# Loads of q and k in rows of eight tokens, longer zero matmuls, and new engine choices and orders

## The chip, the cores and the metric

The kernel runs on one core of a Trainium2 chip. Its engines work side by side, each through its own list of instructions in order: PE (TensorE, matrix products; PEld is its weight load), DVE (VectorE), ACT (ScalarE), POOL (GpSimd) and SP (SyncE, which here issues nearly all DMAs). They meet through semaphores. The metric is the device time of one execution in microseconds (us); lower is better. A profiled execution gives the durations; "span" is the time from its first to its last instruction.

## The reference

Two layers, one behind the other, with B = 4 batches, H = 8 heads, S = 768 tokens, D = 64:

```python
scores = q @ k.T / sqrt(D)                   # per batch and head
keep = (pos_k < 4) | ((0 <= pos_q - pos_k) & (pos_q - pos_k < 128))
a = softmax(where(keep, scores, -1e9))       # 4 sink keys and a window of 128
x = (a @ v), heads side by side              # [B, S, 512]
x_prev = x shifted by one token, zero first
xk = mu_k * x + (1 - mu_k) * x_prev          # xr likewise with mu_r
kk = relu(xk @ w_k) ** 2                     # 512 -> 1024
out = sigmoid(xr @ w_r) * (kk @ w_v)         # [B, S, 512]
```

Inputs and outputs are float32; products run in bfloat16 and sum in float32.

## The kernel before

**Units.** The work is cut into 12 units of 256 tokens: unit u is batch u // 3 and third T = u % 3. A unit goes through four stages, each a function that records operations:

- `load(u, ...)`: SP fetches q, k and v of a unit, float32. k of units 5 to 11 (`KD`) and q of units 8 to 11 (`QD`) come in two DMAs of 256 KB (line 411), to be transposed later by a DMA (line 624); v likewise in two (line 401). The other q and k come in one DMA of 512 KB (line 418; unit 0 in halves), partition p holding tokens 2p and 2p + 1 of each head, 512 bytes a row.
- `prepare(u)`: casts of q, k, v to bfloat16 (kb, qb, vb: lines 607, 610, 658), transposes of kb and qb on PE into a PSUM bank (line 636), and eviction of that bank to kt and qt (line 644). For the first third of a batch also the sink keys (line 675, POOL) and sink values (lines 681, 685).
- `attend(u)`: sink scores (702) and their exponentials es (709), scores (732) in tiles of 64x64, exponentials e (804, ACT), mask (818, DVE), products with v (837), sink products in 64-row tiles (790) or 128-row form (775), reciprocal (851) and normalisation into x (854).
- `mix(u)`: transpose of x (878) and its copy to xt (887), difference td (905), and xk, xr (916, DVE).
- `ffn(u)`: xk @ w_k (968), relu into rl (978 on ACT, 982 on DVE), its square kk (990), the gate product (999) with its tanh th (1005), kk @ w_v (1017), the gated result ob (1026) and its store by SP (1033).

Weights come as float32 and are cast once (572, 576, 578): w_k in four quarters, w_r in two, w_v in four.

**Order.** Every stage records operations with numbers; nothing is issued then. `CHOICE` names by number the engine of those that can run on more than one (casts, evictions, relu; also the form of the sink products). `ORDER` is a list of numbers for each engine. `Plan.schedule` walks these five lists, always taking the head that its small model of the times can start first, and hands out buffers from pools of fixed size (three ob, three ks, qs, vs and so on) in that order. So the order on each engine is that of the list, and the model decides only which buffer goes to whom and where PE gets zero matmuls (`P.fill`, line 1037), put in where the model has PE idle in the first 22 us:

```python
while t - now > (300.0 if now > 4000.0 else 600.0) and now < self.fill_until:
    ...
    order.append(("fill", self.pools["bank"][b[1]]))
```

Of the kernel before, what the change touches and what calls it, by code (L numbers as in the profile page):

```python
# [8 lines left out]
FP32 = mybir.dt.float32  # L9
BF16 = mybir.dt.bfloat16  # L10
# [8 lines left out]
    79: "ACT", 80: "POOL", 81: "POOL", 82: "ACT", 85: "ACT", 88: "ACT", 94: "DVE", 95:  # L19
    "DVE", 97: "DVE", 98: "DVE", 100: "DVE", 102: "ACT", 133: "DVE", 134: "POOL", 136:  # L20
    "DVE", 140: "ACT", 141: "DVE", 159: "PE/tiles", 171: "PE/full", 182: "POOL", 185:
    "DVE", 187: "DVE", 191: "POOL", 194: "DVE", 195: "DVE", 197: "DVE", 212: "DVE",
    216: "DVE", 241: "PE/full", 253: "PE/full", 272: "DVE", 273: "POOL", 276: "DVE",
    348: "DVE", 350: "DVE", 354: "POOL", 357: "ACT", 360: "DVE", 404: "PE/tiles", 416:
    "PE/full", 432: "POOL", 434: "POOL", 437: "ACT", 438: "ACT", 484: "PE/full", 496:
    "PE/tiles", 514: "POOL", 517: "DVE", 518: "ACT", 523: "DVE", 588: "DVE", 593:
    "POOL", 596: "ACT", 597: "ACT", 643: "PE/full", 655: "PE/tiles", 674: "ACT", 675:
    "ACT", 677: "DVE", 721: "PE/tiles", 733: "PE/tiles", 744: "DVE", 746: "POOL", 750:
    "POOL", 752: "ACT", 753: "ACT", 758: "DVE", 823: "DVE", 829: "ACT", 830: "ACT",
    839: "DVE", 876: "PE/tiles", 888: "PE/full", 907: "ACT", 927: "DVE", 952:  # L30
    "PE/full", 964: "PE/full", 1003: "DVE", 1023: "DVE", 1027: "DVE",
# [10 lines left out]

BEGIN = {"SP": 800.0, "PE": 1260.0, "ACT": 800.0, "DVE": 930.0, "POOL": 930.0}
# [3 lines left out]
TOGETHER = 2  # L47

# [63 lines left out]
    ),  # L112
    "ACT": (
# [14 lines left out]
    ),  # L128
    "POOL": (
        74, 76, 72, 71, 73, 75, 101, 103, 134, 191, 80, 81, 182, 273, 354, 278, 277,  # L130
        434, 432, 358, 514, 593, 519, 746, 750, 754, 908,
    ),
# [8 lines left out]
    ),  # L141
}

# [949 lines left out]
```

## Time and profile before

| What | Value |
|---|---|
| median of 3 runs | 169.32 us (169.09 to 169.59) |
| the profiled execution, its own time | 168.63 us |
| its span | 166.9 us |
| granted clock of PE | 0.999 |
| busy in the span: PE, DVE, ACT, POOL | 155.0, 152.4, 126.2, 21.6 us |
| HBM read, written | 24.12 MB, 6.29 MB |

A line of a group reads: source line, engine, operation, tiles written <- tiles read, shapes, xcount | busy us, mean ns of one | idle time of the engine before them and what ended it. A line of the timeline: start us, duration us, engine, line, operation, and in brackets the idle time before it. A merged row (xN) covers N neighbours. "SPq" is SP's queue issuing a DMA. A line of waits: who waited for whom, total us, times, longest us. A line of the windows: the stretch, its length, busy us of each engine with the number of instructions, granted clock, DMA share and GB/s. Slices are equal parts of the span, or of the window asked for; a digit is the busy share in tenths.

### The profile page before, as it was taken

Reading aid. Unit: us, or ns where it says so; the run is one execution under the profiler, and the core shown is the slowest. Engines: PE = TensorE matmul, PEld = TensorE weight load, DVE = VectorE, ACT = ScalarE, POOL = GpSimd, SP = SyncE. Lnnn points to the kernel's source line nnn. Section 1 sums busy time; section 2 is a strip of 40 time slices with the busy share of each in tenths; the row PEclk is TensorE's granted clock in tenths of the full one; section 3 lists DMA queues with packets and bytes.
Section 4 is the critical chain, followed back from the end, with each engine's and each line's share of the span. In section 5 each row is a group of like instructions: output and inputs, shape, how many; then the busy total and the mean of one; then the engine's idle time right before and its main releaser. Section 6 shows DMA issues by size and latency. Waiting matters only on the chain.

```text
span 166.9 us, 4753 instructions
## 1 busy us (share of the span) xinstructions
PE 155.0 (93%) x1870; PEld 102.7 (62%) x1890; DVE 152.4 (91%) x394; ACT 126.2 (76%) x207; POOL 21.6 (13%) x46
## 2 busy tenths in 40 slices
PE   7878948999999999999999999999999999999991
PEld 2436536755757667678566776775666584777441
DVE  6489998999999999999999999999999979999831
ACT  4398974999899899998999878787779658454110
POOL 5532231002133110040004002000000100000000
PEclk9999999999999999999999999999999999999999
DMA  4999989999998999997799799999697881310033
GB/s 134 236 283 346 342 209 390 340 258 302 254 251 171 185 241 264 249 174 183 191 247 213 154 300 195 145 271 217 132 229 128 261 110 64 130 63 0 0 137 114
DMA packets 80725, 33.85 MB, mean 203 GB/s; under 512 B 61624, under 2 KB 75200, under 8 KB 80704
## 3 DMA queue, kind: packets, MB, share of 16 engines
q1 hardware_dynamic: 80688, 33.56, 85.6%
q8 instruction: 14, 0.23, 0.6%
q14 instruction: 7, 0.06, 0.1%
q10 hardware_dynamic: 16, 0.00, 0.0%
HBM read 24.12 MB, written 6.29 MB: 182 GB/s over the span
## 4 chain that ended last, share of the span: by engine, by line
PE 66%; DVE 16%; DMA 6%; SPq 6%; ACT 2%; issue 2%; DVEq 0%
PE bank L968 20%; PE bank L1017 19%; PE bank L999 10%; DMA w<-in_moe_w_k_dram 6%; PE bank L837 6%; PE sc L732 4%; SPq L418 3%; DVE e L818 3%; DVE xr L916 2%; PE bank L878 2%; DVE xk L916 2%; DVE x L854 2%; SPq L401 2%; DVE kk L990 2%; DVE ob L1026 1%
## 5 line engine op out<-in xcount | busy, mean ns | idle before, releaser
L968 PE MATMUL bank<-xk,wk_sb 128*128 128x256 bf16 x384 | 49.3, 273 | 2.0 <-ACT wk_sb L572 1.7
L804 ACT ACTIVATE e<-sc 128x1024 bf16<-128x1024 f32 (+1 forms) x48 | 45.1, 971 | 2.4 <-PE sc L732 2.1
L1017 PE MATMUL bank<-wv_h,kk 128*128 128x512 bf16 x170 | 44.7, 379 | 0.8 <-issue 0.2
L968 PEld LDWEIGHTS <-wk_sb 128*128 128x128 bf16 x384 | 35.9, 98 | 10.4 <-ACT wk_sb L572 2.2
L978 ACT ACTIVATE rl<-bank 128x512 bf16<-128x512 f32 x42 | 24.3, 614 | 12.2 <-PE bank L968 9.7
L818 DVE TENSOR_TENSOR e<-e,mask 128x1024 bf16<-128x1024 bf16 (+1 forms) x48 | 30.3, 645 | 0.4 <-ACT e L804 0.3
L1017 PEld LDWEIGHTS <-kk 128*128 128x128 bf16 x184 | 16.7, 98 | 14.6
L999 PE MATMUL bank<-wr_sb,xr 128*128 128x512 bf16 x90 | 23.7, 379 | 0.3
L916 DVE SCALAR_TENSOR_TENSOR xr<-td,mu_all,xt 128x256 bf16<-128x256 bf16 x48 | 23.2, 498 | 0.0
L916 DVE SCALAR_TENSOR_TENSOR xk<-td,mu_all,xt 128x256 bf16<-128x256 bf16 x48 | 22.7, 500 | 0.0
L990 DVE TENSOR_TENSOR kk<-rl 128x512 bf16<-128x512 bf16 x48 | 19.7, 417 | 1.4 <-ACT rl L978 1.4
L1005 ACT ACTIVATE th<-bank 128x512 f32<-128x512 f32 x24 | 14.7, 623 | 8.0 <-PE bank L999 7.9
L854 DVE TENSOR_TENSOR x<-bank,rec 128x256 bf16<-128x256 f32 x48 | 19.5, 415 | 0.3
L1026 DVE SCALAR_TENSOR_TENSOR ob<-th,bank 128x512 f32<-128x512 f32 x23 | 15.6, 680 | 2.8 <-PE bank L1017 2.0
L837 PE MATMUL bank<-vb,e 128*128 128x65 bf16 x352 | 15.8, 193 | 0.4 <-DVE e L818 0.3
L837 PEld LDWEIGHTS <-e 128*128 128x128 bf16 x352 | 13.9, 97 | 2.8 <-DVE e L818 0.6
L999 PEld LDWEIGHTS <-xr 128*128 128x128 bf16 x96 | 9.0, 98 | 9.0 <-DVE xr L916 0.4
L887 ACT COPY xt<-bank 128x512 bf16<-128x512 bf16 x16 | 9.5, 592 | 5.9 <-PE bank L878 5.4
L732 PE MATMUL sc<-qt,kt 64*64 64x128 bf16 (+3 forms) x512 | 12.6, 227 | 0.2 <-ACT kt L644 0.2
L732 PEld LDWEIGHTS <-kt 64*64 64x64 bf16 x512 | 9.0, 107 | 4.6 <-issue 3.2
L905 DVE TENSOR_TENSOR td<-xt 128x512 bf16<-128x512 bf16 x24 | 10.5, 437 | 0.0
L1037 PE MATMUL bank<-warm 128*128 128x512 bf16 x25 | 8.5, 497 | 1.1 <-DVE warm L1056 1.1
(74 smaller groups left out, 156.9 us busy)
## 6 DMA issues: line engine op xcount, KB each, us to landing
vs<-in_v_dram SPq DMA_DIRECT2D x24, 256.0 KB, 5.4
out_dram<-ob SPq DMA_DIRECT2D x23, 256.0 KB, 3.3
ks<-in_k_dram SPq DMA_DIRECT2D x16, 256.0 KB, 4.3
qs<-in_q_dram SPq DMA_DIRECT2D x7, 512.0 KB, 7.0
qs<-in_q_dram SPq DMA_DIRECT2D x10, 256.0 KB, 4.7
ks<-in_k_dram SPq DMA_DIRECT2D x4, 512.0 KB, 7.3
w<-in_moe_w_k_dram SPq DMA_DIRECT2D x2, 1024.0 KB, 9.4
w<-in_moe_w_v_dram SPq DMA_DIRECT2D x2, 1024.0 KB, 12.7
```

The costliest lines, as they stand in the source:

```text
L732: nc.tensor.matmul(out=sc[keys, a, o0 + f0 - q0:o0 + f1 - q0], lhsT=lhs[rows, keys], rhs=qs[rows, f0:f1], start=u not in BIAS, stop=True, ...
L804: nc.scalar.activation(out=buf[ek][:, :, lo:], in_=buf[sck][:, :, lo:], func=AF.Exp, scale=scale)
L818: nc.vector.tensor_tensor(out=at, in0=at, in1=m, op=ALU.mult)
L837: nc.tensor.matmul(out=o[:, g, a, :], lhsT=e[:, a, e0:e0 + 128], rhs=rhs, start=(T == 0 and i == 0), stop=(i == len(blocks) - 1), skip_gro ...
L854: P.op("DVE", dve(256), lambda ok=ok, rk=rk, c=c: nc.vector.tensor_tensor(out=buf["x", u][:, :, 128 * c:128 * c + 128].rearrange("p g (a d ...
L916: nc.vector.scalar_tensor_tensor(out=buf[key][:, c, :], in0=buf[tk][:, i, :], scalar=mu[w][:, c:c + 1], in1=xt[:, c, t0 - 1:t0 + 255], op0 ...
L968: nc.tensor.matmul(out=ps[:, i, :], lhsT=wk_sb[:, c, 128 * f:128 * f + 128], rhs=xk[:, c, :], start=(c == 0), stop=(c == NC - 1), skip_gro ...
L978: nc.scalar.activation(out=buf[rk], in_=buf[psk].rearrange("p (i t) -> p i t", i=2), func=AF.Relu)
L990: P.op("DVE", dve(512, 0.52), lambda f2=f2, rk=rk: nc.vector.tensor_tensor(out=buf["kk", u][:, 2 * f2:2 * f2 + 2, :], in0=buf[rk], in1=buf ...
L999: nc.tensor.matmul(out=buf[psk], lhsT=buf["xr", u][:, c, 128 * g:128 * g + 128], rhs=wr_sb[:, c, :], start=(c == 0), stop=(c == NC - 1))
L1017: nc.tensor.matmul(out=buf[psk], rhs=wv_h[:, f, :], lhsT=buf["kk", u][:, f, 128 * g:128 * g + 128], start=(f == 0), stop=(f == NF - 1))
L1026: P.op("DVE", dve(512), lambda psk=psk, tk=tk, bk=bk: nc.vector.scalar_tensor_tensor(out=buf[bk], in0=buf[tk], scalar=1.0, in1=buf[psk], o ...
```

## The change

**Rows of eight tokens.** For q and k of units 1 to 11 that are not transposed by DMA (k of units 1 to 4, q of units 1 to 7), partition p now holds 8 neighbouring tokens of two heads: 2048 bytes a row, 256 rows a DMA instead of 1024. The casts, the transposes and the evictions follow that layout; an eviction now writes four of every eight tokens of all four head pairs, where it wrote all tokens of two head pairs, so scores read both halves.

```diff
+OCT = range(1, 12)
+WHOLE = (0,)
...
+            if octet(name, u):
+                P.op("SP", 655.0, lambda key=key, src=src: nc.sync.dma_start(
+                    out=octets(buf[key]).rearrange("p h j d -> p h (j d)"),
+                    in_=src[b, :, 256 * T:256 * T + 256, :].rearrange(
+                        "(i h) (p j) d -> p i h (j d)", j=8, h=2)), rank, service=1420.0,
+                    descs=272, take=[(name + "s", key)], writes=[(name, u, c) for c in range(2)])
+                continue
...
+                        nc.tensor.transpose(
+                            out=ps[:, j, :], identity=ident,
+                            in_=eights(buf[rk])[:, 4 * half + j].rearrange("p h d -> p (h d)"))
...
+                        out=buf[key].rearrange("p c g t -> p c (g t)").rearrange(
+                            "p c (t j) -> p c t j", j=8)[:, :, :, 4 * half:4 * half + 4],
+                        in_=buf[psk].bitcast(BF16)[:, 0:512].rearrange(
+                            "p (j t c) -> p c t j", j=4, c=NP))
...
-            if by_dma(name[0], w):
+            if by_dma(name[0], w) or octet(name[0], w):
                 return [(name, w, 0), (name, w, 1)]
```

**Unit 0's scores** take all 128 keys in one matmul (two row tiles side by side) instead of 64 and 64:

```diff
-                parts = [(slice(0, 64), q0, q1), (slice(64, 128), q0, q1)]
+                parts = [(slice(0, 128), q0, q1)] if u in WHOLE else [
+                    (slice(0, 64), q0, q1), (slice(64, 128), q0, q1)]
```

**Zero matmuls.** Where the model has room, one float32 matmul of 256 or 512 columns stands for two or four of the old ones; 25 become 9 of the old kind and of the float32 kind with 512 columns together, and 6 with 256:

```diff
+        if wide == 1:
+            nc.tensor.matmul(out=bank, lhsT=warm[:, 0:128], start=True, stop=True,
+                             rhs=warm.unsqueeze(1).to_broadcast([128, 2, 256]))
+        else:
+            nc.tensor.matmul(out=bank[:, 0:128 * wide], lhsT=zeros, start=True, stop=True,
+                             rhs=zeros.unsqueeze(1).to_broadcast([128, wide, 128]))
```

**Model, choices, orders.** The model of `Plan.schedule` gets other costs (POOL casts 650 ns, 0.58 of a POOL cast's time blocking DVE), SP held while more than 1600 rows are in flight, and DMAs late by 1300 ns behind 15 listed times (`FETCH`):

```diff
+                while fetch and fetch[0] < slow:
+                    if fetch.pop(0) >= begun - last:
+                        slow += 1300.0
...
+                    if queued + n > 1600.0:
+                        gone = max(given, b1 - (b1 - b0) * (1600.0 - queued) / n)
+                        break
```

`CHOICE` and `ORDER` are replaced whole. Counted by engine, before and after:

| Operation | ACT | DVE | POOL |
|---|---|---|---|
| cast kb | 19, 10 | 2, 1 | 3, 13 |
| cast qb | 11, 12 | 5, 0 | 8, 12 |
| cast vb | 15, 5 | 5, 4 | 4, 15 |
| eviction kt | 7, 7 | 3, 3 | |
| eviction qt | 11, 14 | 5, 2 | |
| copy xt | 16, 17 | 6, 5 | |
| cast w_k | 2, 1 | 0, 1 | 2, 2 |
| cast w_r | 0, 1 | 2, 0 | 0, 1 |
| cast w_v | 2, 2 | 2, 2 | |
| relu | 42, 42 | 6, 6 | |

Of the sink products, 36 matmuls in the 128-row form become 24, and 56 in 64-row tiles become 80. The DMAs are the same in number.

More of the change, by code (lines that the diff above doesn't have):

```diff
@@ L18 @@
 CHOICE = {
[L19 to L31, printed above, removed]
+    79: "ACT", 80: "POOL", 81: "POOL", 83: "POOL", 84: "ACT", 86: "ACT", 88: "ACT",
+    89: "POOL", 91: "DVE", 95: "POOL", 97: "DVE", 101: "DVE", 134: "POOL", 137:
+    "POOL", 140: "ACT", 141: "DVE", 143: "DVE", 159: "PE/full", 171: "PE/tiles", 182:
+    "POOL", 185: "POOL", 191: "POOL", 193: "DVE", 194: "ACT", 220: "DVE", 241:
+    "PE/tiles", 253: "PE/full", 264: "DVE", 270: "POOL", 276: "DVE", 289: "DVE", 297:
+    "DVE", 351: "POOL", 353: "DVE", 354: "POOL", 356: "DVE", 387: "DVE", 404:
+    "PE/full", 416: "PE/tiles", 427: "POOL", 429: "POOL", 432: "POOL", 434: "POOL",
+    440: "DVE", 484: "PE/tiles", 496: "PE/tiles", 509: "POOL", 586: "POOL", 591:
+    "POOL", 643: "PE/tiles", 655: "PE/full", 668: "POOL", 672: "POOL", 721:
+    "PE/tiles", 733: "PE/tiles", 746: "POOL", 752: "ACT", 753: "ACT", 823: "POOL",
+    825: "POOL", 827: "POOL", 830: "DVE", 832: "DVE", 876: "PE/tiles", 888: "PE/full",
+    899: "POOL", 903: "POOL", 908: "ACT", 952: "PE/tiles", 964: "PE/full", 983: "DVE",
+    1019: "DVE", 1023: "DVE", 1031: "DVE",
 }
@@ L41 @@
 LOW = -30000.0
+FETCH = (17500.0, 28500.0, 36900.0, 47800.0, 57300.0, 66500.0, 78000.0, 85500.0,
+         96000.0, 104000.0, 113000.0, 126000.0, 135000.0, 147000.0, 161000.0)
 BEGIN = {"SP": 800.0, "PE": 1260.0, "ACT": 800.0, "DVE": 930.0, "POOL": 930.0}
@@ L85 @@
     "DVE": (
[26 rows of a table removed]
[25 rows of a table added]
     ),
     "ACT": (
[14 rows of a table removed]
[13 rows of a table added]
     ),
     "POOL": (
-        74, 76, 72, 71, 73, 75, 101, 103, 134, 191, 80, 81, 182, 273, 354, 278, 277,
-        434, 432, 358, 514, 593, 519, 746, 750, 754, 908,
[4 rows of a table added]
     ),
     "SP": (
[7 rows of a table removed]
[7 rows of a table added]
     ),
@@ L213, in schedule @@
         clock, port, dma, flying, mode = dict(BEGIN), {}, 0.0, [], 0
+        slow, gone, fetch = 0.0, 0.0, list(FETCH)
         released = {key: 0.0 for key in owner}
@@ L254, in schedule @@
             if o["port"]:
-                port[o["engine"]] = t + cost
+                port[o["engine"]] = t + (0.58 * cost if o["engine"] == "POOL" else cost)
             end = t + cost + o["lag"]
             if o["service"]:
-                descs = o["descs"] if o["engine"] != "POOL" else -10 ** 6
-                flying = [(e, n) for e, n in flying if e > t]
-                over = sum(n for _, n in flying) - o["room"]
-                k = 0
-                while over > 0 and k < len(flying):
-                    over -= flying[k][1]
-                    clock[o["engine"]] = max(clock[o["engine"]], flying[k][0] - 300.0)
-                    k += 1
-                dma = max(dma, t + o["lag"]) + o["service"]
-                end = dma + 100.0
-                if o["service"] > 100.0:
-                    end += next(late for until, late in FUDGE if dma < until)
-                flying.append((dma, max(descs, 0)))
+                given = max(t + cost, gone)
+                clock[o["engine"]] = max(clock[o["engine"]], given)
+                service, ready = o["service"], given + o["lag"] - cost
+                last = service * (0.75 if slow > dma + 200.0 else 1.0)
+                dma, begun = max(dma, ready) + service, max(slow, ready)
+                slow = begun + last
+                while fetch and fetch[0] < slow:
+                    if fetch.pop(0) >= begun - last:
+                        slow += 1300.0
+                slow = max(slow, dma)
+                flying = [f for f in flying if f[1] > given]
+                flying.append((max(slow - last, begun), slow, o["descs"]))
+                queued, gone = 0.0, given
+                for b0, b1, n in reversed(flying):
+                    if queued + n > 1600.0:
+                        gone = max(given, b1 - (b1 - b0) * (1600.0 - queued) / n)
+                        break
+                    queued += n
+                if gone > given + 50.0 and dma < gone + 900.0:
+                    dma = min(slow, gone + 900.0)
+                end = slow + 100.0
+                if service > 100.0:
+                    late = next(late for until, late in FUDGE if slow < until)
+                    end = 100.0 + max(dma + late, slow + late - 300.0)
             o["start"], o["end"] = t, end
@@ L281, in schedule @@
                     free["bank"].remove(b)
-                    now += 225.0 if now > 4000.0 else 430.0
+                    one = 225.0 if now > 4000.0 else 430.0
+                    wide = next((k for k in (4, 2) if t - now > k * one + 75.0), 1)
+                    now += wide * one
                     free["bank"].append((now, b[1]))
-                    order.append(("fill", self.pools["bank"][b[1]]))
+                    order.append(("fill", self.pools["bank"][b[1]], wide))
             order.append(i)
@@ L304, in run @@
             if isinstance(i, tuple):
-                self.fill(i[1])
+                self.fill(*i[1:])
             else:
@@ L392, in by_dma, with octet, octets @@
         return u in (KD if name == "k" else QD)
+    def octet(name, u):
+        return u in OCT and not by_dma(name, u)
+    def octets(t):
+        return t.rearrange("p h j d -> p (h j d)").rearrange("p (h j d) -> p h j d", h=2, j=8)
     def load(u, names, rank, h0=0, h1=H):
@@ L596, with eights @@
              (slice(None), slice(2 * j, 2 * j + 2)), 11 + i, [("wv", i)])
+    def eights(t):
+        return t.rearrange("p j h d -> p (j h d)").rearrange("p (j h d) -> p j h d", h=2, j=8)
     def prepare(u, rank):
@@ L605, in cast @@
             def cast(copy, raw=raw, rk=rk, hs=hs, half=half, name=name):
+                if octet(name, u):
+                    js = slice(4 * half, 4 * half + 4)
+                    return lambda: copy(
+                        out=eights(buf[rk])[:, js].rearrange("p j h d -> p h j d"),
+                        in_=octets(buf[raw])[:, :, js, :])
                 if by_dma(name, u):
@@ L616, in prepare @@
                        "DVE": (dve(512, 0.52), cast(nc.vector.tensor_copy), True),
-                       "POOL": (850.0, cast(nc.gpsimd.tensor_copy), True)},
+                       "POOL": (650.0, cast(nc.gpsimd.tensor_copy), True)},
                  take=[] if half else [(name + "b", rk)],
@@ L630, in prepare, with transpose @@
                 continue
-            def transpose(half=half, psk=psk, rk=rk):
+            def transpose(half=half, psk=psk, rk=rk, name=name):
                 ps = buf[psk].bitcast(BF16)[:, 0:512].rearrange("p (j t) -> p j t", j=4)
                 for j in range(4):
+                    if octet(name, u):
+                        nc.tensor.transpose(
+                            out=ps[:, j, :], identity=ident,
+                            in_=eights(buf[rk])[:, 4 * half + j].rearrange("p h d -> p (h d)"))
+                        continue
                     c = 2 * half + j // 2
@@ L641, in prepare, with evacuate @@
                  reads=["ident", rk + (half,)], writes=[psk], hold=[rk])
-            def evacuate(copy, half=half, psk=psk, key=key):
+            def evacuate(copy, half=half, psk=psk, key=key, name=name):
+                if octet(name, u):
+                    return lambda: copy(
+                        out=buf[key].rearrange("p c g t -> p c (g t)").rearrange(
+                            "p c (t j) -> p c t j", j=8)[:, :, :, 4 * half:4 * half + 4],
+                        in_=buf[psk].bitcast(BF16)[:, 0:512].rearrange(
+                            "p (j t c) -> p c t j", j=4, c=NP))
                 return lambda: copy(
@@ L648, in evacuate @@
                         "p (c j t) -> p c t j", c=2, j=2))
-            P.op("ACT", 600.0, evacuate(nc.scalar.copy), rank + half,
-                 alts={"ACT": (600.0, evacuate(nc.scalar.copy), False),
+            P.op("ACT", 490.0 if octet(name, u) else 580.0, evacuate(nc.scalar.copy), rank + half,
+                 alts={"ACT": (490.0 if octet(name, u) else 580.0, evacuate(nc.scalar.copy), False),
                        "DVE": (625.0, evacuate(nc.vector.tensor_copy), False)},
@@ L658, in cast @@
                 return lambda: copy(out=buf["vb", u][:, g, :, 0:D], in_=buf["v", u][:, g, :, :])
-            P.op("POOL", 850.0, cast(nc.gpsimd.tensor_copy), rank,
-                 alts={"POOL": (850.0, cast(nc.gpsimd.tensor_copy), True),
+            P.op("POOL", 650.0, cast(nc.gpsimd.tensor_copy), rank,
+                 alts={"POOL": (650.0, cast(nc.gpsimd.tensor_copy), True),
                        "ACT": (act(512), cast(nc.scalar.copy), False),
@@ L759, in attend @@
                 P.op("PE", (180.0 if T else 166.0) * TOGETHER,
-                     mode=3,
+                     mode=1 if u in WHOLE else 3,
                      emit=lambda cs=cs: [scores(i) for i in cs], rank=r, lag=PE_LAG,
@@ L1035, in ffn, with fill @@
             P.op("SP", 400.0, store, rank, hold=[bk], reads=[bk], service=800.0)
-    P.fill = lambda bank: nc.tensor.matmul(out=bank, lhsT=warm[:, 0:128], start=True,
-                                           rhs=warm.unsqueeze(1).to_broadcast([128, 2, 256]),
-                                           stop=True)
+    zeros = warm.bitcast(FP32)
+    def fill(bank, wide):
+        if wide == 1:
[4 more added lines that the diff above has]
+                             rhs=zeros.unsqueeze(1).to_broadcast([128, wide, 128]))
+    P.fill = fill
     P.fill_until = 22000.0
```

138 rows, old and new, of the table ORDER are left out of this document.

## The prediction

> **What bounds the kernel now.** I read the page first, then the chain that ended last, the busy time by windows, the waits of TensorE alone, and the timeline where these point.
>
> ```profile
> span 166.9 us, 4753 instructions
> PE   7878948999999999999999999999999999999991
> ## 4 chain that ended last, share of the span: by engine, by line
> PE 66%; DVE 16%; DMA 6%; SPq 6%; ACT 2%; issue 2%; DVEq 0%
> ```
>
> TensorE (PE) ends last and is full in every slice but those of the first 30 us. The windows say whether another engine is as full there:
>
> ```profile
> core 0: us, PE busy (x) PEld busy (x) DVE busy (x) ACT busy (x) POOL busy (x), PEclk, DMA share, GB/s
> 10.00:20.00 10.00, 7.94 (x138) 5.25 (x138) 9.65 (x25) 9.25 (x16) 3.07 (x5) 1.00 1.12 344
> 20.00:30.00 10.00, 7.08 (x119) 5.43 (x118) 9.18 (x24) 6.45 (x12) 1.99 (x2) 1.00 0.99 300
> 30.00:40.00 10.00, 9.80 (x98) 6.24 (x97) 10.00 (x26) 10.00 (x17) 0.00 (x0) 1.00 1.09 296
> 90.00:100.00 10.00, 9.95 (x130) 7.05 (x129) 10.00 (x28) 8.27 (x15) 0.00 (x0) 1.00 0.99 231
> ```
>
> PE loses 2.06 and 2.92 us in the windows from 10 and 20, and 0.2 after that; VectorE (DVE) is full from 30 to 120; GpSimd (POOL) is nearly idle. PE's waits from 30.6 us to 164 are all in these two lines:
>
> ```profile
> PE bank L837 <- DVE e L818: 0.3, 1, 0.3
> PE bank L1017 <- issue: 0.2, 1, 0.2
> ```
>
> So from 30.6 us on the time is the sum of PE's work. A gain must come from the first 30 us; a loss can come from anywhere. What holds PE early, from the chain (first line) and the timeline:
>
> ```profile
> 11.48 10.23 DMA w<-in_moe_w_k_dram
> 21.77 1.38 POOL L578 CAST wk_sb<-w 128x1024 bf16<-128x1024 f32 x1 [2.79 <-DMA w<-in_moe_w_k_dram]
> 22.85 1.05 PE L968 MATMUL bank<-xk,wk_sb 128*128 128x256 bf16 x8 [1.46 <-ACT wk_sb L572]
> 24.55 0.31 PE L790 MATMUL bank<-vsink,es 64*64 64x130 bf16 x8 [0.65 <-ACT es L709]
> ```
>
> The second half of w_k is issued at 11.48 and lands at 21.7; PE stands 1.46 us until its cast is done, then 0.65 for the sink exponentials of unit 1.
>
> **Loads in rows of 2048 bytes.** Eleven loads of 512 KB (k of units 1 to 4, q of 1 to 7) change from rows of 512 bytes to rows of 2048. The load rate in 0 to 25 us, 0.625 us a slice, holds both kinds:
>
> ```profile
> GB/s 0 0 2 87 302 338 225 211 210 298 286 256 200 150 215 344 319 317 301 292 292 296 320 364 396 380 383 410 370 390 375 295 250 225 124 53 87 334 351 282
> ```
>
> From slice 16 (9.4 us) eight slices average 310 GB/s: q and k of unit 1, q of unit 2, in 512-byte rows. The next eight average 384: w_k, in 2048-byte rows. 524288 bytes take 1.69 us by the first and 1.37 by the second, 0.32 less. Three of these loads stand ahead of w_k on SyncE's queue, before and after, so w_k lands about 1.0 us earlier (ends 0 and 1.2, the latter from the best slices, 410): its halves at 16.8 and 20.7 instead of 17.8 and 21.7. The later loads, beyond that, come 2 us earlier at most; PE waits for none of them (window above), so I count nothing; without that cover nothing gets worse either.
> The Trainium skill's page "DMA: Bandwidth & Descriptors", section Specifications, puts the shortest transfer at line rate at 512 bytes. By that the longer rows bring nothing, and 1.0 us leaves the sum; 310 against 384 GB/s speak against it.
>
> **First product.** It needs the w_k cast on ScalarE (ACT), which ended at 19.34. ACT is busy from 8.6 us to there but for 0.7 us. In the new order it has ahead of that cast, from 8.5 us, four unit-0 exponentials (0.82), two casts (0.63), five q and k evictions (0.60), one x eviction (0.59) and two exponentials (1.05), 10.2 us; so the earlier landing does not help it, and the cast ends at 8.5 + 10.2 + 1.1 = 19.8. The 16 matmuls behind it (0.11 each, some 2 us in the trace) end at 21.8. The last quarter of w_k goes from ACT (1.06) to DVE (0.68, the wr_sb row of the same form), done at 20.7 + 0.7 = 21.4: the 1.46 wait goes. The sink exponentials follow two e exponentials on ACT, with no cast of v ahead of them any more: 19.8 + 2.1 + 0.4 = 22.3; so the sink products start at 22.4, with 4 matmuls (0.44 us) less done than at 24.55 before. Lead: 24.55 - 22.4 - 0.44 = 1.7 us. What is late next is DVE: masks and the relu square, cast of v, then four reciprocals and normalisations (4 x 0.59), which I place at 26.4 instead of 27.7. So 1.3 of the 1.7 us is left.
>
> **Casts to POOL.** Counted in the two instruction orders:
> - DVE: 5 qb, 1 kb, 1 vb casts, 3 qt evictions, 2 wr casts, 1 xt copy less, 1 wk cast more: 7 x 0.42 + 3 x 0.68 + 2 x 0.68 + 0.41 - 0.68 = 6.0 us less.
> - ACT: 9 kb and 10 vb casts less (19 x 0.63), one qb, three qt, one xt more: some 9 us less.
> - POOL: 25 casts more (10 kb, 4 qb, 11 vb) and a wr cast: 25 x 0.61 to 1.13 (the shortest and longest row of one), 16 to 29 us on top of 21.6; it stays under half the span.
>
> ```profile
> L610 DVE CAST qb<-qs 128x512 bf16<-128x512 f32 x4 | 1.7, 415 | 0.0
> L644 DVE COPY qt<-bank 128x512 bf16<-128x512 bf16 x5 | 3.4, 679 | 2.9 <-PE bank L636 2.9
> L658 POOL CAST vb<-vs 128x512 bf16<-128x512 f32 x4 | 3.0, 743 | 35.7 <-DMA vs<-in_v_dram 35.7
> ```
>
> But a POOL cast delays DVE. Beside two POOL casts that run from 87.64 for 1.76 us:
>
> ```profile
> 88.09 0.83 DVE L916 SCALAR_TENSOR_TENSOR xr<-td,mu_all,xt 128x256 bf16<-128x256 bf16 x1
> 88.85 0.83 DVE L905 TENSOR_TENSOR td<-xt 128x512 bf16<-128x512 bf16 x1
> 89.60 0.47 DVE L916 SCALAR_TENSOR_TENSOR xr<-td,mu_all,xt 128x256 bf16<-128x256 bf16 x1
> ```
>
> xr takes 0.47 alone and 0.83 beside a cast. Over the whole trace, the 15 casts of 512 columns cost DVE 2.4 us over the clear durations of the same forms (8 casts hit an operation with two SBUF inputs, 0.30 each; 7 hit none; operations that read PSUM are not delayed), 0.16 a cast; the two w_k casts 0.39 each. 25 x 0.16 + 0.39 = 4.4 us come back. DVE ends 1.6 us lighter, and as PE is full from 30.6 on, that is worth nothing there by itself; it keeps the new order supplied.
>
> **PE's own work.** Counts of products, value matmuls and transposes are unchanged. Of unit 0's scores 32 matmuls on 64 keys become 16 on 128; two run side by side instead of four, with equal columns in all: nothing. Sink products: 12 of 128 rows less, 24 of 64 rows more, three groups at 0.22 (4 x 56 ns) become groups of 8 in 4-way tiles, 0.11 to 0.24: 0 to 0.3 us less, I take 0.2. Changes of tile shape (93 ns each in the trace) go from 60 to 63: 0.3 us more. 25 zero matmuls become 15, longer ones; no row shows the float32 kind. Between one (0.22) and four passes (0.86) a 512-column one lies under PE's idle time before 19.4; the last stands right before the first product and can hold it by 0.43 at the worst, or by nothing.
> **Evictions** with 8-byte output runs: taken at the old 0.60 (ACT) and 0.68 (DVE); 0.1 either way times 17 before 30 us is in the range. Scores of units 1 to 7 now wait for both halves of k and q; in the order PE reaches them after both, nothing. **SyncE**: one issue of k with its 1024 rows held it for 4.29 us; with 256 it is held less and loads are queued earlier; the issues stay 115. On its queue, store 480 (ob of unit 3) moves among the last transposes, which parks one of three ob buffers; the old order parks store 322 (unit 1) from unit 1 to unit 4, and no wait of DVE for a store is listed. On POOL's queue the cast of k of unit 2 stands ahead of a w_k quarter and waits for its load; PE needs that quarter only after that k.
>
> **Sum.** Early lead 1.3, sinks 0.2, shapes -0.3, waits after 30.6 as before, and of PE's waits between 26 and 30.6 (1.2 us: 0.38, 0.23, 0.20 and smaller ones) a quarter, since k of unit 2 and x of unit 1 come earlier against an unchanged 24 matmuls: 1.3 + 0.2 - 0.3 + 0.3 = 1.5 us less. The profiled execution took 168.63 (166.9 and 1.7 around it): 167.1. The median of the runs is 169.32, 0.69 above it; the same difference gives 167.8.
>
> **Rivals.**
> 1. *DVE becomes the bound (slower).* Each of the 25 added casts delays one two-input operation by 0.30, and wr by 0.78: 8.3 us against 6.0 removed, so DVE, full from 30 to 120, gets 2.3 us more: 171.6. It decides from 0.23 a cast on ((6.0 - 0.39)/25). For it: eight hits of 15, and DVE is full; casts that come in pairs hit more. Against it: 0.16 on average so far. The Trainium skill's page "SBUF — State Buffer", section "SBUF: two separate sides", says the port pair of the two engines is held by one for a whole instruction and the other is blocked; the 0.83 us rows agree.
> 2. *Row length does nothing.* Then w_k lands as before, the last quarter is cast at 22.4 instead of 22.8, and 0.4 is left: 168.9. It is the case that the Trainium skill's DMA page, above, would have.
> 3. *The new order meets new waits in the full stretch.* The old one loses 0.5 us in 133; the early stretch shows what a missed link costs (1.46, 0.65, 0.38). Three such, 2.5 us, against the 1.5: 170.3.
> 4. *All early waits vanish*: PE's waits between 21 and 30.6 sum to 3.5 us; with the sinks, 165.6.
>
> **How the numbers follow.** Forecast 0.46, rival 1 0.16, rival 2 0.11, rival 3 0.17, rival 4 0.10. About 0.3% (0.5 us) is what a measurement of this kernel can tell from no change. Rival 2 sits at that edge and is split. Faster: 0.44 of the forecast, 0.10 and 0.04; same: 0.07 and the forecast's upper edge of 0.02; slower: 0.16 + 0.17. The range takes rival 4 to most of rival 1: 165.2 to 171.4. The forecast's own range is 166.6 to 168.6.
>
> **What would show it.** Right: w_k's second landing near 20.7, no wait of a microsecond between the first product and the sink products, these near 22 us, and PE without waits after 31. Wrong: load slices still near 310 GB/s; xr and xk above 0.55 us on average (now 0.50), and PE waiting for DVE after 31 us; SyncE waiting for POOL casts ahead of transposes, or DVE for an ob buffer.

## The result, and the profile after

| | ratio to the kernel before | 95% interval |
|---|---|---|
| first comparison | 0.994 | 0.9911 to 0.9969 |
| repeated (experiment 5) | 0.9998 | 0.996 to 1.0037 |
| repeated (experiment 11) | 1.0046 | 1.0009 to 1.0083 |

The median of the first four executions was 170.28 us (168.14 to 172.30), against 169.27 us (169.09 to 169.59) for the kernel before. The ratios leave out executions more than 1.5% above the fastest of their own kernel, which over all comparisons were 11 of 28 of the changed kernel and 5 of 84 of the other; so the first ratio rests on two executions. The three together say that the change is worth less than half a per cent, in no direction that can be named. The predicted gain, 167.8 against 169.32, is a ratio of 0.991: the first interval just touches it, the other two do not hold it. The stated range, 165.2 to 171.4, holds all three, but it also holds a kernel that gains nothing.

The profiled execution took 168.71 us (before 168.63). From its page, the span, TensorE's busy share by slice, the busy times, and the chain that ended last:

```profile
span 167.0 us, 4752 instructions
PE 155.6 (93%) x1865; PEld 103.7 (62%) x1884; DVE 151.0 (90%) x382; ACT 119.1 (71%) x193; POOL 41.0 (25%) x72
PE   7687998999999999999989999999999999999991
...
DVE 45%; PE 43%; issue 5%; DMA 3%; SPq 1%; ACT 1%; DVEq 0%; ACTq 0%
```

PE's sixth slice (21 to 25 us) holds 9 tenths where it held 4, but the twenty-first (84 to 88 us) has gone from 9 to 8, and the chain that ended last, 66% PE and 16% DVE before, now runs as much through DVE as through PE. In the windows each engine has its busy time and, in brackets, its instructions:

```profile
core 0: us, PE busy (x) PEld busy (x) DVE busy (x) ACT busy (x) POOL busy (x), PEclk, DMA share, GB/s
10.00:20.00 10.00, 8.51 (x130) 5.77 (x127) 9.51 (x24) 8.81 (x14) 4.01 (x8) 1.00 1.08 366
20.00:30.00 10.00, 9.18 (x136) 7.32 (x134) 9.94 (x25) 8.84 (x16) 3.22 (x4) 1.00 0.99 285
70.00:80.00 10.00, 9.39 (x142) 6.84 (x142) 9.93 (x26) 8.18 (x15) 3.19 (x4) 1.00 1.11 206
80.00:90.00 10.00, 9.41 (x104) 6.18 (x103) 9.90 (x26) 7.76 (x14) 3.97 (x7) 1.00 0.84 193
```

From 20 to 30 us PE is busy 2.1 us more than before (7.08). From 70 to 90 it is busy 0.9 us less (9.78 and 9.89), in windows where DVE is full. The load rate, 0 to 25 us in slices of 0.625 us:

```profile
GB/s 0 0 0 105 311 347 253 234 277 296 274 227 147 176 143 410 406 387 393 393 370 383 357 387 397 393 400 396 396 308 282 214 184 192 292 363 251 169 187 269
```

From 9.4 us the eight slices that averaged 310 GB/s before average 387: q and k of unit 1 and q of unit 2 now run as w_k does. The timeline of the first stretch:

```profile
19.89 1.91 PE L1022 MATMUL bank<-xk,wk_sb 128*128 128x256 bf16 x16
21.28 0.68 DVE L612 CAST wk_sb<-w 128x1024 bf16<-128x1024 f32 x1
22.02 0.61 PE L1022 MATMUL bank<-xk,wk_sb 128*128 128x256 bf16 x4 [0.23 <-DVE wk_sb L612]
22.47 0.39 PE L829 MATMUL bank<-vsink,es 128*128 128x130 bf16 x4
27.85 0.36 PE L786 MATMUL sc<-qt,kt 64*64 64x192 bf16 x10
```

The wait for the cast of w_k's last quarter is 0.23 us (1.46 before), that for the sink exponentials is gone, and the scores of unit 2 start at 27.85 instead of 29.28: a lead of 1.4 us. At the end of PE's work nothing of it is left (163.64 against 163.58). TensorE's waits behind 30.6 us, the two largest:

```profile
PE bank L844 <- DVE ob L1080: 0.6, 1, 0.6
PE bank L1022 <- DVE x L908: 0.5, 1, 0.5
```

Before, the largest wait there was 0.3 us. Both are for DVE.

### The profile page after: what moved, and what is told of

Same layout as the page of the kernel before. It is cut to its first block, busy times and chain, and to the rows that moved or that the text cites. A ratio compares the mean times of both kernels' runs of the same rounds, so it can differ in the third digit from the quotient of the medians.

```text
span 167.0 us, 4752 instructions
## 1 busy us (share of the span) xinstructions
PE 155.6 (93%) x1865; PEld 103.7 (62%) x1884; DVE 151.0 (90%) x382; ACT 119.1 (71%) x193; POOL 41.0 (25%) x72
## 4 chain that ended last, share of the span: by engine, by line
DVE 45%; PE 43%; issue 5%; DMA 3%; SPq 1%; ACT 1%; DVEq 0%; ACTq 0%
PE bank L1071 14%; PE bank L1022 12%; DVE e L872 10%; PE bank L1053 7%; DVE xr L970 6%; DVE xk L970 5%; DVE x L908 5%; DVE kk L1044 4%; PE bank L891 3%; DMA vs<-in_v_dram 3%; DVE ob L1080 3%; DVE td L959 3%; PE sc L786 2%; DVE rec L905 2%; PE bank L932 1%
## 5 line engine op out<-in xcount | busy, mean ns | idle before, releaser
L1022 PE MATMUL bank<-xk,wk_sb 128*128 128x256 bf16 x384 | 51.4, 273 | 1.1 <-DVE x L908 0.5
L1022 PEld LDWEIGHTS <-wk_sb 128*128 128x128 bf16 x384 | 35.4, 98 | 10.1 <-issue 1.2
L1032 ACT ACTIVATE rl<-bank 128x512 bf16<-128x512 f32 x42 | 24.9, 607 | 15.9 <-PE bank L1022 14.0
L872 DVE TENSOR_TENSOR e<-e,mask 128x1024 bf16<-128x1024 bf16 (+1 forms) x48 | 32.5, 691 | 0.1
L970 DVE SCALAR_TENSOR_TENSOR xk<-td,mu_all,xt 128x256 bf16<-128x256 bf16 x48 | 22.4, 496 | 0.1
L891 PE MATMUL bank<-vb,e 128*128 128x65 bf16 x352 | 16.8, 194 | 1.7 <-DVE e L872 1.4
L711 POOL CAST vb<-vs 128x512 bf16<-128x512 f32 x15 | 12.7, 854 | 15.4 <-DMA vs<-in_v_dram 15.3
L941 ACT COPY xt<-bank 128x512 bf16<-128x512 bf16 x17 | 10.0, 588 | 4.4 <-PE bank L932 4.4
L786 PE MATMUL sc<-qt,kt 64*64 64x128 bf16 (+4 forms) x496 | 12.8, 226 | 0.2
L786 PEld LDWEIGHTS <-kt 64*64 64x64 bf16 (+1 forms) x496 | 9.2, 106 | 4.0 <-issue 2.1
L649 POOL CAST qb<-qs 128x512 bf16<-128x512 f32 x5 | 3.7, 755 | 28.1 <-PE bank L1022 13.0
```

The costliest lines, as they stand in the source:

```text
L786: nc.tensor.matmul(out=sc[keys, a, o0 + f0 - q0:o0 + f1 - q0], lhsT=lhs[rows, keys], rhs=qs[rows, f0:f1], start=u not in BIAS, stop=True, ...
L872: nc.vector.tensor_tensor(out=at, in0=at, in1=m, op=ALU.mult)
L891: nc.tensor.matmul(out=o[:, g, a, :], lhsT=e[:, a, e0:e0 + 128], rhs=rhs, start=(T == 0 and i == 0), stop=(i == len(blocks) - 1), skip_gro ...
L970: nc.vector.scalar_tensor_tensor(out=buf[key][:, c, :], in0=buf[tk][:, i, :], scalar=mu[w][:, c:c + 1], in1=xt[:, c, t0 - 1:t0 + 255], op0 ...
L1022: nc.tensor.matmul(out=ps[:, i, :], lhsT=wk_sb[:, c, 128 * f:128 * f + 128], rhs=xk[:, c, :], start=(c == 0), stop=(c == NC - 1), skip_gro ...
L1032: nc.scalar.activation(out=buf[rk], in_=buf[psk].rearrange("p (i t) -> p i t", i=2), func=AF.Relu)
```

## The experiments

Each ratio is to the kernel before, timed on the same chip.

**1. New orders, old rows.**

```diff
-OCT = range(1, 12)
+OCT = ()
```

> The changed kernel with its orders, choices and zero matmuls, but q and k loaded in the old 512-byte rows. If the longer rows carry the early lead, the second half of w_k lands 1.0 to 1.9 us later than 19.87, the scores of unit 2 (27.85 in the changed kernel, 29.28 before) start 0.8 to 1.4 us later, and the time goes from about 168.4 to 169.2 to 169.8, level with the kernel before (ratio 0.999 to 1.003). If the orders carry it, the time stays near 168.4 (ratio 0.993 to 0.997).

Measured: 1.028 (1.0223 to 1.0336), span 173.0 us. The loss is larger than expected, and it is not where w_k lands: that was at 21.36 (19.87 in the changed kernel), but DVE came to the cast at 21.50 (21.28) and the sink products started at 22.68 (22.47), 0.2 us later. It comes later. TensorE's waits behind 30.6 us, and DVE's from 30 to 60:

```profile
PE bank L1080 <- DVE vsink L796: 1.6, 1, 1.6
PE bank L1129 <- DVE wv_h L668: 1.0, 1, 1.0
```

```profile
DVE wv_h L668 <- DMA w<-in_moe_w_v_dram: 1.3, 1, 1.3
```

At 39 us DVE stands in order before a cast of w_v whose load is not there, and PE stands behind it for 1.0 us. k of unit 3 lands at 36.59 us instead of 33.67, q of unit 3 at 40.95 instead of 38.84. The longest wait, 1.6 us at 73 us, stands behind a DVE that is full there and waits for no load; what made it late was not traced. These waits do not cover the loss of this profile: all idle time of PE from 30 to 164 us sums to 3.8 us, against 2.9 in the changed kernel, and a fall of the granted clock (0.70 and 0.62 in the two windows of 2.5 us from 75 us on) is worth some 1.7 us, by an estimate from these figures; the rest was not located. The loss is not the clock's alone, since executions with a mean clock of 0.998 or more took 172.74 to 174.34 us. So the ratio shows that the new orders need the loads at the pace of the long rows; by which waits they lose is shown only in part.

**2. Zero matmuls of the old kind alone.**

```diff
-                    wide = next((k for k in (4, 2) if t - now > k * one + 75.0), 1)
+                    wide = 1
```

> The changed kernel with each long float32 zero matmul replaced by as many of the old kind as the model has room for. If the long ones only cover idle time, the same time within 0.2 us (ratio 0.993 to 0.997) and the same clock. If they hold the first product (the last one ran from 19.35 to 20.05, the first product started at 19.89, its w_k cast ended at 19.72), the first product starts 0.1 to 0.2 us earlier and the time falls by at most as much.

Measured: 1.0036 (0.9998 to 1.0074), among the ratios of the changed kernel itself: the kind of zero matmul makes no difference to the time that this shows. In its profile the first product starts 0.08 us after the end of its w_k cast, against 0.17 in all three profiles of the changed kernel.

**3. The new start, the old order behind it.** What the changed kernel starts in the first 28 us, with its order and engines, and behind it the rest in the old order on the old engines; rows of 2048 bytes throughout. The edit is in `CHOICE` and `ORDER` alone, for example DVE from its 53rd operation:

```diff
-        201, 220, 243, 297, 248, 217,
+        225, 217, 201, 209, 83, 84,
...
```

> New orders and choices for the operations that the model starts in the first 28 us, and behind them the operations in the old orders with the old choices (one transpose of unit 3 moved up one place, so that scores find both halves); rows of 2048 bytes throughout. If the early lead of 1.4 us is real and the new order gives 1.0 us of it back later in waits for VectorE, this keeps it: ratio 0.988 to 0.993 (167.3 to 168.0). If the old order cannot use the lead (its own waits grow), 0.995 to 1.002.

Measured: 1.0182 (1.0135 to 1.0229). TensorE's waits from 28 to 60 us:

```profile
PE bank L1112 <- ACT rl L1091: 2.4, 1, 2.4
PE sc L845 <- DVE kt L751: 1.5, 1, 1.5
```

The two halves do not fit: PE waits 2.4 us at 32 us for a relu on ScalarE and 1.5 us at 46 us, with scores, for an eviction of k, 3.9 us together. The worth of the new start alone could not be had this way.

**4. Twenty casts of units 5 to 11 back on ScalarE**, each at the place in its order where GpSimd had started it:

```diff
-427: "POOL", 429: "POOL", 509: "POOL", 586: "POOL",
+427: "ACT", 429: "ACT", 437: "ACT", 438: "ACT",
...
-    "ACT": (... 402, 335, 340, 375,
+    "ACT": (... 402, 427, 335, 429, 340, 375,
```

> The changed kernel with 20 casts of units 5 to 11 (those that it moved from ScalarE to GpSimd) back on ScalarE, each at the place where GpSimd ran it; nothing else moved but one load and one copy by one place. If casts on GpSimd delay VectorE and this makes TensorE's waits after 40 us, VectorE loses 20 x 0.16 = 3.2 us of busy time, these waits (2.4 us) go back to the 1.5 of before and the time falls by 0.5 to 1.0 us (ratio 0.988 to 0.992). If the waits come from the order alone, no change (0.993 to 0.997). If ScalarE becomes late by the 12.6 us of work put on it, slower than the changed kernel by 0.5 us or more, with waits of TensorE for ScalarE.

Measured: 1.0115 (1.0066 to 1.0165), slower. With 20 casts on GpSimd instead of 40 the time rises. ScalarE has 20 casts of 0.6 us more among its evictions and exponentials. That this hides what DVE gets back is likely but not shown; so the price of a cast on GpSimd cannot be read from this run, and giving the casts back is no remedy.

**5. The changed kernel once more**, unaltered.

> The changed kernel itself, unaltered, measured on the chip on which the next three run, to place their ratios. If its gain is a property of the kernel, the ratio to the kernel before is about 0.994 again (0.991 to 0.997). If the gain is of the size by which two measurements of one kernel differ, the ratio is within 0.3% of 1, and so it is for the zero-matmul variant, which came out at 1.0036.

Measured: 0.9998 (0.996 to 1.0037): the second case of the expectation. Span 168.0 us, 1.0 more than the first profile. TensorE's waits from 60 us on:

```profile
PE bank L844 <- DVE ob L1080: 0.6, 1, 0.6
PE bank L1022 <- DVE x L908: 0.5, 1, 0.5
PE bank L891 <- DVE e L872: 0.4, 1, 0.4
```

The first two stand where they stood in the first profile; they belong to the order, not to one execution. The third is new here.

**6. Long rows on the old order.** The changed code with the old `CHOICE` and `ORDER`, four operations moved so that scores find both halves of k and q:

```diff
 PE:   288,
-323, 271, 319
+271, 323, 319
 ACT:  239,
-242, 247, 190, 85
+190, 242, 247, 85
 DVE:  208,
-248, 221, 243, 86
+221, 86, 248, 243
```

> The changed code (rows of 2048 bytes, unit 0's scores whole, long zero matmuls) with the engine choices and the orders of the kernel before; four operations of the old orders stand one or two places later so that scores find both halves of q and k. Theory 'the new order is what turns faster loads into time': w_k's halves land about 1 us earlier here too, but the last quarter's cast stays on ScalarE behind its old neighbours, so TensorE's 1.46 us wait shrinks only in part: gain 0 to 0.6 us, ratio 0.997 to 1.000. Rival 'any early landing is a gain of its own': the wait of 1.46 and that of 0.65 us vanish here as well: ratio 0.988 to 0.993. Rival 'each order fits only the loads that it was found with': new waits of a microsecond each appear behind 30 us: ratio 1.005 to 1.02.

Measured: 1.017 (1.0111 to 1.023): the last rival by the ratio. w_k's first quarter is cast from 15.95 us, earlier than in either kernel, and that earns nothing. TensorE's waits:

```profile
PE sc L849 <- DVE kt L755: 2.5, 2, 1.4
PE sc L849 <- ACT kt L755: 1.5, 1, 1.5
```

Scores that could start on the first half of k now wait for the eviction of the second: 4 us in three waits, one of them ahead of 30 us and so not where the rival put it. This is the price of the new layout; the new order, which puts both evictions early, has no such wait.

**7. The same twenty casts to GpSimd on the old order**, rows of 512 bytes:

```diff
-437: "ACT", 438: "ACT",
+427: "POOL", 429: "POOL", 437: "POOL", 438: "POOL",
...
-    "POOL": (... 278, 277, 434,
+    "POOL": (... 278, 427, 277, 429, 434,
```

> The kernel before, with 512-byte rows and its own order, but the casts of units 5 to 11 that the change gives to GpSimd (20 of 512 columns) moved there from ScalarE. Theory 'a GpSimd cast costs VectorE 0.15 us on average': VectorE loses 20 x 0.15 = 3.0 us and, as it is full from 30 to 120 us, TensorE waits for up to that much: ratio 1.005 to 1.018. Rival 'VectorE has slack of that size beside TensorE': TensorE gets no new waits, ratio 0.997 to 1.003. Rival of the prediction with 0.23 us or more a cast: 4.6 us or more, ratio above 1.02.

Measured: 1.0248 (1.0198 to 1.0297), 4.2 us for 20 casts, 0.21 each: the last rival by the ratio, and close to the 0.23 from which the prediction's rival 1 decides. From the page, busy times, and TensorE's waits behind 30.6 us:

```profile
PE 157.0 (91%) x1870; PEld 103.3 (60%) x1890; DVE 156.9 (91%) x394; ACT 117.5 (68%) x187; POOL 38.6 (22%) x66
```

```profile
PE bank L911 <- POOL vb L732: 1.6, 2, 1.4
```

DVE, with the same operations, is busy 4.5 us longer (152.4 before). But PE also waits 1.6 us for casts of v that GpSimd delivers late. Experiment 10 tells the two apart in part.

**8. Long rows for units 1 and 2 alone.**

```diff
-OCT = range(1, 12)
+OCT = (1, 2)
```

> The changed kernel with rows of 2048 bytes for q and k of units 1 and 2 alone (four loads of the eleven); q and k of units 3 to 7 come in 512-byte rows again, as all did in the first experiment, which was 2.8% slower than before. Theory 'the long rows earn by w_k's earlier landing alone': w_k lands at 19.9 as in the changed kernel and the early stretch is the same; q and k of units 3 and 4 land up to 1.5 us later, which costs nothing: ratio 0.994 to 0.998. Rival 'the new order also needs its later loads early': waits of TensorE of 0.5 to 2 us in the stretch from 30 to 80 us: ratio 1.005 to 1.02.

Measured: 1.0173 (1.0123 to 1.0223): the rival. Against experiment 5 on the same chip, the long rows of the seven loads of units 3 to 7 are worth 1.75%, 3 us.

**9. Narrow casts, new order.** Of the 40 casts of 512 columns on GpSimd 22 (10 of v, 7 of k, 5 of q) are cut to 16 columns; the kernel leaves out the other columns, so part of q, k and v does not reach the result:

```diff
+            def tiny(raw=raw, rk=rk, half=half):
+                return nc.gpsimd.tensor_copy(out=buf[rk][:, half, 0, 0:16],
+                                             in_=buf[raw][:, 4 * half, 0, 0:16])
...
-                       "POOL": (650.0, cast(nc.gpsimd.tensor_copy), True)},
+                       "POOL": (650.0, tiny if by_dma(name, u) else
+                                cast(nc.gpsimd.tensor_copy), True)},
...
-            P.op("POOL", 650.0, cast(nc.gpsimd.tensor_copy), rank,
+            P.op("POOL", 650.0, tiny if u > 4 else cast(nc.gpsimd.tensor_copy), rank,
```

> The changed kernel with some 24 of its 40 GpSimd casts of 512 columns (those of v from unit 5 on, and of k and q that go on to a transposing DMA) cut to 16 columns; the other values of these tiles stay what they were, so part of q, k and v is left out. Orders, waits and engines are unchanged: what goes is the time of those casts and their hold on VectorE's port. Theory 'the port is what takes the gain back': VectorE's delays beside casts fall from 5.8 to 7.0 us to 2.5 to 4, VectorE's busy time falls by about 3 us, TensorE's waits for VectorE behind 30 us shrink to under 1 us, and the spread between executions closes: ratio 0.983 to 0.990. Rival 'the port costs nothing that the end sees': ratio 0.994 to 1.000, as the changed kernel has it, with the same waits.

Measured: 0.9949 (0.9915 to 0.9984), against 1.0046 (1.0009 to 1.0083) for the changed kernel in the same comparison: 1.0%, 1.6 us for 22 casts, 0.07 each. Its profiled execution lost time before 13 us, where the granted clock was 0.6 for one slice, and its first product starts only at 21.45 us. From 60 us on no wait of TensorE over 0.15 us is left, and all of them sum to 0.8 us, against 2.1, 2.4 and 2.1 us in the three profiles of the changed kernel; the waits for `ob` and `x` are gone. But from 30 to 60 us it has two waits for DVE that no profile of the changed kernel has:

```profile
PE bank L1031 <- DVE xk L979: 1.0, 1, 1.0
PE bank L900 <- DVE x L917: 0.9, 1, 0.9
```

With them its waits from 30 to 164 us sum to 3.0 us, no less than in the changed kernel; whether they follow from the late start was not found out. From the 33rd product with w_k to the end of PE's work it takes 134.7 us in spite of these waits, the changed kernel 135.3, 136.1 and 135.8, the kernel before 133.8 and 134.2. So the gain of 1.0% is shown by the times, and the waits show only where a part of it lies. In the three profiles of the changed kernel no matmul and no instruction of DVE waits for a cast on GpSimd behind 30 us, so casts that merely end sooner are no obvious rival to the delay of DVE. The theory's price was missed: the ratio is 0.5% above what it gave and by itself would suit the rival; the delay, counted as in the table below, is 4.6 us (2.5 to 4 expected), DVE is busy 150.1 us, 0.9 to 2.0 less (3 expected), and the spread between executions did not close (167.25 to 171.21 us).

**10. Narrow casts, old order.** The same cut in the kernel of experiment 7.

> The same cut (16 columns) in the kernel before with 20 casts given to GpSimd, which was 2.5% slower than before at full width. Theory 'its loss is the port': with the delays gone the time falls back to that of the kernel before or, since ScalarE stays relieved of 20 casts, a little below: ratio 0.990 to 1.000. Rival 'its loss is GpSimd delivering late or the moved neighbours of the order': the cut makes the casts shorter but leaves the place of each behind its load: ratio 1.008 to 1.025, with TensorE still waiting for vb of GpSimd.

Measured: 1.0051 (1.0017 to 1.0085), between the two cases of the expectation. Against 1.0248, 2.0% or 3.3 us of the 4.2 are gone. From the page, busy times, and the wait for the casts of v:

```profile
PE 155.7 (92%) x1870; PEld 103.4 (61%) x1890; DVE 152.3 (90%) x394; ACT 117.6 (69%) x187; POOL 27.0 (16%) x66
```

```profile
PE bank L920 <- POOL vb L740: 0.7, 1, 0.7
```

DVE is back at 152.3 us; its delay, counted as in the table below, falls from 7.2 to 2.4 us. The wait for v has shrunk by 0.9 us as well, so by an estimate from one profile each some 2.4 of the 3.3 us are DVE's delay, 0.11 us for each of the 22 casts, and the rest lateness. The 0.9 us of loss that remain were not told apart; beside the wait for v, waits of 0.7 us for a relu on ScalarE and of 0.6 us for a transposing DMA of q are in the profile, which the kernel before does not have.

**11. The changed kernel a third time, and 12. the kernel before, unaltered.**

> The changed kernel itself once more, for a third profile of it and a third ratio. Theory 'executions of one kernel differ by how many GpSimd casts meet an operation of VectorE with two operands in SBUF': so far 5.8 us of delay went with a span of 167.0 and 7.0 us with 168.0; a third profile lies near that line (each us of delay 0.6 to 1 us of span). Rival 'the span differs for another cause': delay and span do not go together. The ratio: 0.994 to 1.000.

> The kernel before, unaltered, profiled on this chip beside the three others. Its ratio to itself shows what this measurement can tell: 0.997 to 1.003. Its delays beside GpSimd casts, 3.2 us in the first profile, should be within 0.8 us of that if 15 casts leave less to chance than 40 do, and its span within 0.6 us of 166.9.

Measured: 1.0046 (1.0009 to 1.0083) and 0.9972 (0.9938 to 1.0006). So this measurement tells about half a per cent from nothing, not the 0.3% that the prediction took. All five profiles side by side ("delay" is the time of e, kk, td, xk and xr over their clear durations wherever they ran beside a GpSimd instruction; "waits" is the sum of all of TensorE's, small ones included):

| | before | before (12) | changed | changed (5) | changed (11) |
|---|---|---|---|---|---|
| span, us | 166.9 | 166.7 | 167.0 | 168.0 | 167.7 |
| first product | 19.39 | 19.14 | 19.89 | 19.81 | 19.52 |
| sink products | 24.55 | 23.93 | 22.47 | 22.70 | 22.71 |
| 33rd product with w_k | 29.75 | 29.10 | 28.31 | 28.54 | 28.55 |
| waits, 30 to 164 us | 1.75 | 1.50 | 2.86 | 3.12 | 2.41 |
| DVE busy | 152.4 | 152.5 | 151.0 | 152.1 | 152.0 |
| delay by GpSimd | 3.2 | 3.3 | 5.8 | 7.0 | 6.6 |

In the old kernel the delay repeats to 0.1 us; in the changed one it runs from 5.8 to 7.0, and the span goes with it, 0.8 us a us. Three points are few, and the same executions differ elsewhere too.

## Why the prediction was right and where it was not

The early lead came as forecast; the forecast time did not. That the first comparison comes near it, with a ratio of 0.994, is largely luck: it rests on two executions, and two longer comparisons give 0.9998 and 1.0046. The lead is given back behind 30 us, where the prediction counted nothing.

**Loads.** Right in rate (384 expected, 387 measured), and w_k's second half landed at 19.87 (20.68 and 20.55 in the other two profiles), against 20.7. The Trainium skill's page "DMA: Bandwidth & Descriptors", section Specifications, would have both row lengths at line rate; 310 and 387 GB/s speak against that for these loads. But the step, and rival 2 with it, gave most of the lead to the rows. Experiment 1 shows that they bring 0.2 us of it at the sink products and 0.4 at the 33rd product with w_k (28.74 against 28.31): with 512-byte rows DVE casts the last quarter 0.2 us later, because DVE is busy until then anyway. So most of the lead comes from the order, by the waits that are gone: the last quarter is cast on DVE, and the sink exponentials have no cast ahead of them.

**The later loads, counted as nothing.** Wrong for the new order. PE waited for none of them in the old kernel, but experiments 1 and 8 show 1.7 to 2.8% lost when they come at the old pace, for one part (1.0 us in experiment 1) by a DVE that stands in order behind a load. It did not enter the result, since the change brings rows and orders together; it means that neither part can be priced alone. Experiment 6 shows the other side: that scores lose nothing by waiting for both halves holds only in the new order; in the old one it costs 4 us of waits, and the run is 2.9 us longer.

**First product.** Right: 19.89 (19.8), its 16 matmuls end at 21.80 (21.8), sink products at 22.47 (22.4), lead at the scores of unit 2 1.4 us (1.3). It starts 0.17 us after the cast on ScalarE, 0.05 before; with the old kind of zero matmul (experiment 2) it is 0.08, so the long ones cost about 0.1, under the bound of 0.43.

**Casts to GpSimd.** The term of 4.4 us was 2.6 to 3.8 (the delay of 5.8 to 7.0 less 3.2), and DVE ended 0.3 to 1.4 us lighter instead of 1.6. The step that failed is the next one, "waits after 30.6 as before". With the small ones they sum to 2.86, 3.12 and 2.41 us against 1.75 (the prediction's 0.5 counted the two listed ones alone), 0.7 to 1.4 more, most of it for DVE, and two waits stand at the same places each time. That is rival 3's mechanism (new waits in the full stretch) at about half its price. Rival 1's mechanism (casts that delay DVE) is behind part of it. From the timeline of the changed kernel, GpSimd and then DVE ahead of the wait for `x` that starts at 85.6 us:

```profile
83.68 1.17 POOL L649 CAST qb<-qs 128x512 bf16<-128x512 f32 x2 [0.76 <-DMA qs<-in_q_dram]
```

```profile
84.24 1.28 DVE L970 SCALAR_TENSOR_TENSOR xk<-td,mu_all,xt 128x256 bf16<-128x256 bf16 x2
85.65 0.42 DVE L908 TENSOR_TENSOR x<-bank,rec 128x256 bf16<-128x256 f32 x1
```

Two xk take 0.87 us clear and 1.28 here, and the `x` that PE waits for comes 0.4 us later. Experiment 9 shows the sum: with 22 casts narrow these two waits vanish and 1.6 us come back, though its profile has two others ahead of 60 us. The Trainium skill's page "SBUF — State Buffer", section "SBUF: two separate sides", has the port of DVE and GpSimd held for a whole instruction; DVE's 156.9 and 152.3 us in experiments 7 and 10 agree.

**Sum.** Of the lead of 1.4 us in the first profile 1.1 went into these waits. The other 0.4 us is not idle time of PE; 0.3 would be the changes of tile shape that the prediction counted, which was not measured. The repeated profiles have a lead of 1.2 us and give back 2.3 and 2.0. All these leads are against the first profile of the kernel before; against its second, whose early stretch is 0.6 us shorter, they are 0.6 to 0.8 us. So part of the lead that the prediction saw to be won lay in one execution.

**Rivals and dangers.** Rival 2 fell with the load rate, rival 4 with the waits behind 30 us. No wait of DVE for a store of `ob` and none of PE for the w_k quarter behind k of unit 2 is in the profile, so the parked store and GpSimd's order cost nothing.

**Still open.** The waits for `ob` and `x` go when the casts are narrow; an order that removes them with the casts at full width was not tried. What else in the new order takes back the lead was not told apart from the casts.

## What to carry to other kernels

An order found for one pace of its loads is one piece with that pace: rows, starts and casts taken singly cost 1 to 3% here in either direction, while the whole is worth under half a per cent. A nearly idle GpSimd was not free room beside a full VectorE: a cast of 512 columns cost the run 0.07 us in the new order, and 0.21 in the old one, of which some 0.11 is the delay of VectorE. Where TensorE and VectorE are both full, as here, price the later waits too before counting a lead won at the start. And profile the kernel before twice: its own early stretch differed by 0.6 us between two executions, a good part of the lead in question.

## What the runs showed of the hardware

- Executions of one program differ in how often GpSimd delays VectorE: the operations with two inputs in SBUF lost 5.8, 7.0 and 6.6 us beside GpSimd instructions in three executions of the changed kernel, 0.3 to 0.4 us for each that was hit.
- In experiment 1 the granted clock fell to 0.83 in the window from 70 to 80 us, right behind waits of 0.38 and 1.61 us that ended at 73.0 and 74.9 us. In experiment 3 a wait of 2.4 us was followed by no such fall (mean clock 0.998), so what decides it stays open.
- An eviction of q into rows of eight tokens took 594 ns on ScalarE and 681 on VectorE, as the old form did (597 and 679), in spite of its 8-byte runs.
